# Window attention and two feed-forward stages on one core: another order in the first block, two float32 groups fewer

## The chip, the core and the metric

One core of a Trainium2 chip. Its engines are TensorE (PE; loads of weights are shown apart as PEld), VectorE (DVE), ScalarE (ACT), GpSimd (POOL) and SyncE (SP), which issues most of the transfers. Each engine works through its own instructions in a fixed order; between engines, semaphores make one wait for another. The metric is device time of the whole program in microseconds, the median of several runs.

## The reference

Attention in a window of 64 positions over 32 heads, then two feed-forward stages:

```python
scores = scale * np.matmul(q, k.transpose(0, 1, 3, 2))
mask = (rel >= 0) & (rel < window)          # rel = row - column, window = 64
attn = softmax of scores where mask, row by row
x = (attn @ v), heads side by side          # 2304 x 512
a = x @ w1                                  # 512 x 1024
b = x @ w2                                  # 512 x 1024
h = a * b @ w3                              # 1024 x 1024
x = h @ w_out                               # 1024 x 512
h = x @ w_in                                # 512 x 2048
g = h * (1.0 / (1.0 + np.exp(-h)))
return g @ w_out2                           # 2048 x 512
```

The inputs of the first stages come in double words, two 32-bit words for a number, which the kernel turns into float32 itself.

## The kernel before

The kernel writes its order out by hand; no scheduler moves anything. Nearly all of its products run with operands that are split into a high and a low part (hi and lo, a cast and a subtraction), three products for one: hi by hi, hi by lo, lo by hi.

**Phase W** (0 to 84 us) converts the weights and multiplies w3 and w_out into one matrix, which lies as eight split tiles wp[0] to wp[7]. A weight goes through steps (`steps_to`): step t scales chunk t on ACT (L168, L171), joins chunk t-1 on DVE (L200, L203) and POOL (L207), casts the high part of chunk t-3 on ACT (L214) and makes the low part of chunk t-4 (L218) on POOL or DVE. The weights w1 and w2 are the last 16 chunks; the last steps run inside block 0 of phase A. The last four accumulators of phase W (accw) are split into wp[4] to wp[7] by a cast on ACT (L127) and a subtraction on DVE (L130).

**Phase A** (84 to 450 us) has nine blocks of 256 tokens. A block is 288 products. Products 0 to 191 make 16 tiles (tile s: 12 products; ab), four tiles for each of i = 0 to 3: two for a, two for b. ACT copies a out (L739), DVE multiplies it with b (L741), and the product p is split for the pair i: its high part on ACT (L127), its low part on POOL (L130). Products 192 to 287 (x2, L757) multiply p by wp, two accumulators of 48 products each; the lines in the diff call the eight pieces of p f = 0 to 7, two for each i. All accumulators turn through four banks.

Between the products stand the **halves** of the attention, for 72 groups of two heads by 128 rows. In block 0 a half comes at products 9, 33, 57, 81, 105, 123, 141, 159, 177 and on in steps of 18. An even half of group g has the products of the scores of g, of the values of g-2 and the transposes of g-1; an odd half normalises g and prepares group g+2: for a split group a cast of q and k on ACT (L375), the low part of k on POOL (L381, two instructions) and of q on DVE (L387), and for v a cast on ACT (L396) and a low part on POOL (L399). A **plain** group, one with g < PLAIN, has none of this: its scores (L407) and values (L484 to L486) are products in float32. Block 0 begins with the even half of group 12 at its product 9.

`tick` runs before each product: it starts the halves that are due and then the `moves` put down for that product number, the last weight steps among them. `split_x` splits the next block's x. Groups 13 and 14 stand in block 0's halves at products 57 to 159.

Of the kernel before, what the change touches and what calls it, by code (L numbers as in the profile page):

```python
# [14 lines left out]
ALU = mybir.AluOpType  # L15
# [8 lines left out]
NA = 256  # L24
NBLK = T // NA
# [4 lines left out]
PLAIN = 15  # L30
# [13 lines left out]
def tile_window_attention_ffn(ctx, tc, qkv, qkp, vp, w1, w2, w3t, w_out, w_in, w_out2, out):  # L44
# [92 lines left out]
    def accumulator(name, shape):  # L137

        turn[0] = (turn[0] + 1) % converting["banks"]
        return ps.tile(shape, F32, name=name, tag=f"ps{turn[0]}")  # L140
# [568 lines left out]
    def phase_a(blk, hooks):  # L709
# [4 lines left out]
        def unit(n):  # L714
            hooks(n)

        def tick(n):
            n += 288 * blk
            halves_to(W_HALVES + halves_by(n))
            events(n)  # L720

        for s in range(16):
            i, m, j = s // 4, s // 2 % 2, s % 2
            f = 2 * i + j
            unit(s)
            fs = slice((f % 4) * 128, (f % 4 + 1) * 128)
            if j == 0:
                acc = accumulator(f"ab{blk}_{s}", [128, 512])
            for k in range(4):
                w = weights["12", (2 * m + f // 4) * 4 + k]  # L730
                for n, (l, r) in enumerate(PASSES):
                    tick(12 * s + 3 * k + n)
                    nc.tensor.matmul(  # L733
                        acc[:, j * NA : j * NA + NA], lhsT=w[l][:, fs], rhs=x[k // 2][r][:, k % 2],
                        start=(j == 0 and k == 0 and n == 0), stop=(k == 3 and n == 2), skip_group_check=True,
                    )
            if j and m == 0:
                a_sb = slot(f"a{blk}_{i}", "st", [2, 512], bufs=4)
                nc.scalar.copy(out=a_sb[:, 0], in_=acc)  # L739
            elif j:  # L740
                nc.vector.tensor_tensor(out=a_sb[:, 1], in0=acc, in1=a_sb[:, 0], op=ALU.mult)  # L741
                hi, lo = [y[:, 2 * i : 2 * i + 2] for y in p]
                split(hi, lo, a_sb[:, 1].rearrange("p (f n) -> p f n", f=2), "act", "pool")
        for i in range(2):
            acc = accumulator(f"x2_{blk}_{i}", [128, 512])
            early, late = (range(6), (6, 7)) if i == 0 else (range(8), ())
            todo = [(o, f, n) for o in range(2) for f in early for n in ((0, 0), (1, 0), (0, 1))]
            for passes in (((0, 0), (1, 0)), ((0, 1),)):
                todo += [(o, f, n) for o in range(2) for f in late for n in passes]
            for n, (o, f, (l, r)) in enumerate(todo):  # L750
                if n % 12 == 0:
                    unit(16 + 4 * i + n // 12)
                if blk + 1 < NBLK and (i, n) in ((0, 28), (1, 16)):
                    split_x(blk + 1, i)
                tick(192 + 48 * i + n)
                at = (2 * i + o) * 128
                nc.tensor.matmul(  # L757
                    acc[:, o * NA : o * NA + NA], lhsT=wp[f][l][:, at : at + 128], rhs=p[r][:, f],
                    start=(n == 0), stop=((o, f) not in [y[:2] for y in todo[n + 1 :]]), skip_group_check=True,
                )  # L760
            x2 = slot(f"x2s{blk}_{i}", "st", [2, NA], bufs=4)
            nc.scalar.copy(out=x2, in_=acc.rearrange("p (o n) -> p o n", o=2))
            nc.scalar.dma_start(
                out=x2d[2 * i : 2 * i + 2, :, blk * NA : (blk + 1) * NA].rearrange("o p n -> p o n"), in_=x2
            )
# [684 lines left out]
```

## Time and profile before

| | us |
|---|---|
| median of 3 runs | 804.27 (802.56 to 805.58) |
| profiled execution | 803.03 |
| its span, first to last instruction | 800.6 |
| PE busy | 792.2 |
| DVE, ACT, POOL busy | 632.0, 558.3, 346.0 |
| phase W | 0 to 84.2 |
| block 0 of phase A | 84.2 to 128.1 |
| block 1 | 128.1 to 170.0 |

In the trace a row has a start and a duration; matmuls are pipelined and their durations overlap, so the time that a matmul costs is the distance of starts. In brackets stands how long the engine was idle before the row, and what released it.

### The profile page before, as it was taken

To read this page: it belongs to the slowest core of one execution; us is meant where nothing else is said; L and a number is where in the kernel's file an instruction comes from. 1 tells how busy PE (TensorE), PEld (TensorE's weight loads), DVE (VectorE), ACT (ScalarE), POOL (GpSimd) and SP (SyncE) were. 2 spreads that over 40 slices of the span, in tenths; PEclk is the share of its full clock that TensorE was granted. 3 is DMA by queue.
4 is the path that set the end of the run, shared out by engine and by line. 5 is a ranking of instruction groups with operands and counts; after the bars stand their busy time and mean duration, and the time that the engine had idled before them with its cause. 6 is when DMAs were issued, how large, how long until landed. Compare 5 with 4: busy or idle time off the path is not lost.

```text
span 800.6 us, 17243 instructions
## 1 busy us (share of the span) xinstructions
PE 792.2 (99%) x5926; PEld 750.0 (94%) x5926; DVE 632.0 (79%) x1545; ACT 558.3 (70%) x1288; POOL 346.0 (43%) x416
## 2 busy tenths in 40 slices
PE   8999999999999999999999999999999999999998
PEld 4555899999999999999999999999999999999998
DVE  7898677888889888889747777847646899998882
ACT  6998868898988898888845677767657655434440
POOL 5778766777877686878533303433100000000000
PEclk9999999999999999999999999999999999999999
DMA  9998134455536554643413359789675845554421
GB/s 298 366 317 292 57 116 151 139 169 171 167 117 184 160 164 131 181 150 126 160 53 107 126 189 337 255 302 349 239 273 183 293 130 159 160 152 146 133 79 53
DMA packets 81494, 146.77 MB, mean 183 GB/s; under 512 B 7040, under 2 KB 47616, under 8 KB 81408
## 3 DMA queue, kind: packets, MB, share of 16 engines
q1 hardware_dynamic: 76352, 140.80, 54.1%
q10 hardware_dynamic: 5056, 4.88, 1.8%
q8 instruction: 47, 0.77, 0.4%
q14 instruction: 39, 0.32, 0.1%
HBM read 105.81 MB, written 39.85 MB: 182 GB/s over the span
## 4 chain that ended last, share of the span: by engine, by line
PE 84%; DVE 4%; ACT 3%; DMA 2%; issue 1%; SPq 0%; ACTq 0%; DVEq 0%
PE ab L733 23%; PE x L757 12%; PE oa L1197 10%; PE ob L1197 8%; PE ha L1046 6%; PE hd L1046 6%; PE hb L1046 6%; PE hc L1046 3%; PE t L458 3%; PE o L491 1%; PE accw L657 1%; PE s L411 1%; PE s L415 1%; DMA gst<-t 1%; PE o L492 1%
## 5 line engine op out<-in xcount | busy, mean ns | idle before, releaser
L733 PE MATMUL ab<-xb,hl 128*128 128x256 f32 x864 | 132.1, 281 | 0.0
L733 PE MATMUL ab<-xa,hl 128*128 128x256 f32 x864 | 122.1, 277 | 0.1
L733 PEld LDWEIGHTS ab<-xb,hl 128*128 128x128 f32 x864 | 112.1, 188 | 0.1
L733 PEld LDWEIGHTS ab<-xa,hl 128*128 128x128 f32 x864 | 109.4, 188 | 0.9 <-DVE wp L130 0.9
L757 PE MATMUL x<-p,wp 128*128 128x256 f32 x864 | 105.1, 278 | 0.0
L757 PEld LDWEIGHTS x<-p,wp 128*128 128x128 f32 x864 | 100.5, 188 | 0.0
L381 POOL TENSOR_TENSOR klo<-qk,qkhi 64x192 fp32r<-64x192 f32 x114 | 72.1, 632 | 4.5 <-ACT qkhi L375 0.2
L1197 PE MATMUL oa<-wo_w,hi 128*128 128x256 f32 x408 | 73.8, 276 | 0.0
L130 POOL TENSOR_TENSOR p<-a,p 128x512 fp32r<-128x512 f32 x36 | 47.9, 1330 | 38.5 <-ACT p L127 38.2
L1197 PEld LDWEIGHTS oa<-wo_w,hi 128*128 128x128 f32 x408 | 61.6, 188 | 0.0
L1197 PE MATMUL oa<-wo_w,lo 128*128 128x256 f32 x204 | 56.3, 276 | 0.0
L1046 PE MATMUL ha<-xop,wi_w 128*128 128x384 f32 x288 | 54.0, 337 | 0.0
L436 ACT ACTIVATE sm<-sm,nm 128x192 f32<-128x192 f32 x114 | 51.1, 449 | 2.8 <-DVE nm L422 1.2
L1046 PEld LDWEIGHTS ha<-xop,wi_w 128*128 128x128 f32 x288 | 50.1, 188 | 0.4 <-ACT gxa L1068 0.2
L375 ACT CAST qkhi<-qk 128x768 fp32r<-128x768 f32 x57 | 47.6, 835 | 1.3
L914 POOL TENSOR_TENSOR cv_b<-cv_b,cv_r 128x512 int32<-128x512 int32 x16 | 21.6, 1352 | 60.9 <-DVE cv_b L911 46.5
L422 DVE CUSTOM_DVE_ANT_0 sm<-s,consts 128x192 f32<-128x192 f32 x144 | 45.6, 354 | 2.9 <-PE s L415 1.1
L1046 PE MATMUL hd<-xop,wi_w 128*128 128x384 f32 x252 | 47.6, 336 | 0.0
L448 DVE TENSOR_TENSOR sm<-sm,rs 128x384 f32<-128x384 f32 x57 | 45.7, 801 | 1.9
L127 ACT CAST p<-a 128x512 fp32r<-128x512 f32 x36 | 22.4, 621 | 35.5 <-DVE a L741 35.5
L1046 PEld LDWEIGHTS hd<-xop,wi_w 128*128 128x128 f32 x252 | 44.0, 188 | 0.0
L503 POOL TENSOR_TENSOR xr<-ot 128x128 f32<-128x128 f32 x44 | 25.8, 587 | 39.9 <-DVE ot L502 31.4
(282 smaller groups left out, 2167.3 us busy)
## 6 DMA issues: line engine op xcount, KB each, us to landing
qk<-in_qkv SPq DMA_DIRECT2D x57, 384.0 KB, 3.1
gd<-gxa SPq DMA_DIRECT2D x24, 384.0 KB, 4.2
words<-in_w SPq DMA_DIRECT2D x16, 512.0 KB, 7.5
xe<-in_w_in SPq DMA_DIRECT2D x16, 512.0 KB, 5.2
gq<-in_w_out SPq DMA_DIRECT2D x16, 512.0 KB, 5.4
words<-in_w3t SPq DMA_DIRECT2D x15, 512.0 KB, 7.8
gd<-gst SPq DMA_DIRECT2D x18, 384.0 KB, 5.5
xe<-gd SPq DMA_DIRECT2D x13, 512.0 KB, 3.9
```

The source lines that it names most:

```text
L130: (nc.vector if eng_lo == "dve" else nc.gpsimd).tensor_tensor(out=lo, in0=src, in1=f32(hi), op=ALU.subtract)
L375: nc.scalar.copy(out=hi, in_=t)
L381: nc.gpsimd.tensor_tensor(out=k_lo[g % 2][hs, h * 192 : h * 192 + 192], in0=t[hs, n], in1=f32(hi[hs, n]), op=ALU.subtract)
L422: nc.vector.tensor_tensor_reduce(out=sm[g % 2][:, h, :], in0=s_ps[:, h, :], in1=consts[:, at + 64 - 64 * h : at + 256 - 64 * h], op0=ALU.a ...
L436: nc.scalar.activation(out=e[:, h, :], in_=x, func=AF.Exp, scale=-1.0, bias=nm[:, h : h + 1], accum_out=sums_of[g % 2][:, h, 0:1])
L448: nc.vector.tensor_tensor(out=x, in0=e, in1=rs.unsqueeze(2).to_broadcast([128, 2, 192]), op=ALU.mult)
L458: nc.tensor.transpose(t_ps[:, i * 128 : i * 128 + 128], x[:, at : at + 128], id_sb)
L503: nc.gpsimd.tensor_tensor(out=to, in0=t[:, 0:128], in1=t[:, 128:256], op=ALU.add)
L733: nc.tensor.matmul(acc[:, j * NA : j * NA + NA], lhsT=w[l][:, fs], rhs=x[k // 2][r][:, k % 2], start=(j == 0 and k == 0 and n == 0), stop= ...
L757: nc.tensor.matmul(acc[:, o * NA : o * NA + NA], lhsT=wp[f][l][:, at : at + 128], rhs=p[r][:, f], start=(n == 0), stop=((o, f) not in [y[: ...
L1046: nc.tensor.matmul(bank[name][:, q, 0:NB], lhsT=w[:, l, first + kt], rhs=x[:, kt, r, :], start=(fresh and kt == 0 and n == 0), stop=(kt == ...
L1197: nc.tensor.matmul(dst, lhsT=lhs[l], rhs=rhs[r], start=(first and e == 0 and q == 0 and n == 0), stop=(e == DUOS - 1 and q == 1 and n == 2 ...
```

## The change

Float32 groups go from 15 to 13: groups 13 and 14 are split like all that follow. Block 0 does its tiles in two portions: tiles 0 to 7, then the x2 products that need only p of these (48 of 96), then tiles 8 to 15 and the other 48. Both x2 accumulators are then open through the second portion, and its tiles turn through the two banks left. In each portion the x2 products of the second pair come last, first those that read the high part of p (LEFT), then those with its low part (RIGHT). Blocks 1 to 8 keep their order. The seven weight steps of block 0 stand at products 15, 39, 63, 87, 97, 111 and 129 instead of 15, 27, 43, 60, 68, 79 and 107, and the low part of the last goes from DVE to POOL.

```diff
-PLAIN = 15
+PLAIN = 13
...
-    def accumulator(name, shape):
-
-        turn[0] = (turn[0] + 1) % converting["banks"]
+    def accumulator(name, shape, of=(0, 1, 2, 3)):
+
+        turn[0] = of[(of.index(turn[0]) + 1) % len(of)] if turn[0] in of else of[0]
         return ps.tile(shape, F32, name=name, tag=f"ps{turn[0]}")
...
+        def ab_tiles(units, banks=(0, 1, 2, 3)):
+            for s in units:
...
+                for k in range(4):
+                    w = weights["12", (2 * m + f // 4) * 4 + k]
+                    for n, (l, r) in enumerate(PASSES):
+                        tick()
...
+                elif j:
+                    nc.vector.tensor_tensor(out=a_sb[:, 1], in0=acc, in1=a_sb[:, 0], op=ALU.mult)
+                    hi, lo = [y[:, 2 * i : 2 * i + 2] for y in p]
+                    split(hi, lo, a_sb[:, 1].rearrange("p (f n) -> p f n", f=2), "act", "pool")
...
+        def x2_tiles(*todo):
+            for i, o, f, (l, r) in todo:
+                if i not in acc2:
+                    acc2[i] = accumulator(f"x2_{blk}_{i}", [128, 512])
+                tick()
...
+        ALL, LEFT, RIGHT = ((0, 0), (1, 0), (0, 1)), ((0, 0), (1, 0)), ((0, 1),)
+
+        def some(i, fs, passes):
+            return [(i, o, f, n) for o in range(2) for f in fs for n in passes]
+
+        if blk:
+            ab_tiles(range(16))
+            x2_tiles(*some(0, range(6), ALL), *some(0, (6, 7), LEFT), *some(0, (6, 7), RIGHT), *some(1, range(8), ALL))
+            return
+        for g in range(2):
+            f = 4 * g
+            ab_tiles(range(8 * g, 8 * g + 8), (0, 1, 2, 3) if g == 0 else [n for n in range(4) if n not in held])
+            x2_tiles(*some(0, (f, f + 1), ALL), *some(1, (f, f + 1), ALL))
+            held = (turn[0], (turn[0] - 1) % 4)
+            for i in range(2):
+                x2_tiles(*some(i, (f + 2, f + 3), LEFT), *some(i, (f + 2, f + 3), RIGHT))
+        turn[0] = held[0]
...
-        for i, n in enumerate((15, 27, 43, 60, 68, 79, 107)):
-            low = nc.vector if i == 6 else nc.gpsimd
-            moves.setdefault(n, []).append(lambda i=i, low=low: steps_to(W12_B + 25 + i, (low,)))
+        for i, n in enumerate((15, 39, 63, 87, 97, 111, 129)):
+            moves.setdefault(n, []).append(lambda i=i: steps_to(W12_B + 25 + i, (nc.gpsimd,)))
```

How instructions stand on three engines, before and after (the number behind a name is the program's own for the buffer, and line numbers of the changed kernel differ by some).

ACT at the end of phase W, before: the last two chunks are scaled (words), then the four accumulators are cast into wp.

```order
L214 CAST hl<-cv_b 128x512
L168 ACTIVATE cv_b<-words 128x512
L171 ACTIVATE cv_r<-words 128x512
L168 ACTIVATE cv_b<-words 128x512
L171 ACTIVATE cv_r<-words 128x512
L127 CAST wp_971<-accw_0_640 128x512
L127 CAST wp_975<-accw_1_641 128x512
```

The same place on ACT after:

```order
L214 CAST hl<-cv_b 128x512
L168 ACTIVATE cv_b<-words 128x512
L171 ACTIVATE cv_r<-words 128x512
L168 ACTIVATE cv_b<-words 128x512
L171 ACTIVATE cv_r<-words 128x512
L375 CAST qkhi_969<-qk_904 128x768
L127 CAST wp_980<-accw_0_640 128x512
L127 CAST wp_984<-accw_1_641 128x512
```

The cast of q and k of group 13 now stands ahead of the casts of wp.

POOL in block 0, before, up to the low part of p for the second pair (p from a_1): L207 and L218 are sums and low parts of weights, klo the low part of k.

```order
L207 TENSOR_TENSOR cv_b<-cv_b,cv_r 128x512 x2
L218 TENSOR_TENSOR hl<-cv_b,hl 128x512
L207 TENSOR_TENSOR cv_b<-cv_b,cv_r 128x512
L218 TENSOR_TENSOR hl<-cv_b,hl 128x512
L130 TENSOR_TENSOR p_994<-a_0_1049,p_994 128x512
L207 TENSOR_TENSOR cv_b<-cv_b,cv_r 128x512
L218 TENSOR_TENSOR hl<-cv_b,hl 128x512 x3
L381 TENSOR_TENSOR klo_80<-qk_1077,qkhi_1183 64x192 x2
L130 TENSOR_TENSOR p_994<-a_1_1165,p_994 128x512
```

POOL after, from the low part of k of group 14 to the same low part of p:

```order
L381 TENSOR_TENSOR klo_79<-qk_906,qkhi_1073 64x192 x2
L207 TENSOR_TENSOR cv_b<-cv_b,cv_r 128x512
L218 TENSOR_TENSOR hl<-cv_b,hl 128x512
L130 TENSOR_TENSOR p_1003<-a_0_1058,p_1003 128x512
L207 TENSOR_TENSOR cv_b<-cv_b,cv_r 128x512
L218 TENSOR_TENSOR hl<-cv_b,hl 128x512
L381 TENSOR_TENSOR klo_80<-qk_974,qkhi_1182 64x192 x2
L399 TENSOR_TENSOR vhl_1184<-v_1080,vhl_1184 128x3x64
L207 TENSOR_TENSOR cv_b<-cv_b,cv_r 128x512
L218 TENSOR_TENSOR hl<-cv_b,hl 128x512
L130 TENSOR_TENSOR p_1003<-a_1_1167,p_1003 128x512
```

Two low parts of weights have moved behind p; the low parts of a second group's k and of a v have come ahead of it.

PE before, around product 120 (ab_8 and ab_10 are tiles 8 to 11; s, o and t are the scores, values and transposes of the half at product 105):

```order
L733 MATMUL ab_8_1209<-xa_570,hl 128x256 x6
L733 MATMUL ab_8_1209<-xb_833,hl 128x256 x3
L407 MATMUL s_1219<-kq_81 128x384
L484 MATMUL o_1226<-pw_127,vp_83 128x128
L485 MATMUL o_1226<-pw_127,vp_83 128x128
L486 MATMUL o_1226<-pw_127,vp_83 128x64
L458 MATMUL t_1231<-consts,sm_78 128x128 x3
L733 MATMUL ab_8_1209<-xb_833,hl 128x256 x3
L733 MATMUL ab_8_1209<-xa_570,hl 128x256 x6
L733 MATMUL ab_8_1209<-xb_833,hl 128x256 x6
L733 MATMUL ab_10_1257<-xa_570,hl 128x256 x6
```

PE after, from shortly ahead of product 120 (the third row) on:

```order
L759 MATMUL x_0_1_1261<-p_1003,wp_594 128x256 x3
L759 MATMUL x_0_1_1261<-p_1003,wp_598 128x256 x3
L759 MATMUL x_0_0_1219<-p_1003,wp_629 128x256 x2
L759 MATMUL x_0_0_1219<-p_1003,wp_633 128x256 x2
L759 MATMUL x_0_0_1219<-p_1003,wp_629 128x256 x2
L759 MATMUL x_0_0_1219<-p_1003,wp_633 128x256 x2
L759 MATMUL x_0_0_1219<-p_1003,wp_629 128x256
L759 MATMUL x_0_0_1219<-p_1003,wp_633 128x256
L759 MATMUL x_0_0_1219<-p_1003,wp_629 128x256
L759 MATMUL x_0_0_1219<-p_1003,wp_633 128x256
L759 MATMUL x_0_1_1261<-p_1003,wp_629 128x256 x2
```

Where tiles 10 and 11 stood, PE now has x2 products of the second pair: eight with p's high part, then four, from product 128, with its low part.

## Rows read from the trace of the kernel before

**Rows 1.** The page, busy time by engine and granted clock in slices
```profile
PE 792.2 (99%) x5926; PEld 750.0 (94%) x5926; DVE 632.0 (79%) x1545; ACT 558.3 (70%) x1288; POOL 346.0 (43%) x416
...
PE   8999999999999999999999999999999999999998
...
PEclk9999999999999999999999999999999999999999
```

**Rows 2.** The page, chain that ended last, shares by engine
```profile
PE 84%; DVE 4%; ACT 3%; DMA 2%; issue 1%; SPq 0%; ACTq 0%; DVEq 0%
```

**Rows 3.** Timeline of PE, three halves; start us, us, engine, line, instruction
```profile
99.49 0.81 PE L407 MATMUL s<-kq 128*128 128x384 f32 x2
...
101.00 0.60 PE L733 MATMUL ab<-xb,hl 128*128 128x256 f32 x3
...
105.35 0.37 PE L411 MATMUL s<-qkhi 128*128 128x192 f32 x2
...
106.62 0.60 PE L733 MATMUL ab<-xb,hl 128*128 128x256 f32 x3
...
116.27 0.37 PE L411 MATMUL s<-qkhi 128*128 128x192 f32 x2
...
117.27 4.36 PE L757 MATMUL x<-p,wp 128*128 128x256 f32 x36
```

**Rows 4.** Timeline of PE, products 120 to 131 of block 0
```profile
102.81 0.84 PE L733 MATMUL ab<-xa,hl 128*128 128x256 f32 x6
103.49 0.99 PE L733 MATMUL ab<-xb,hl 128*128 128x256 f32 x6
```

**Rows 5.** Timeline of all engines, from phase W to block 0
```profile
82.86 2.01 ACT L127 CAST wp<-accw 128x512 fp32r<-128x512 f32 x4
...
83.45 2.48 DVE L130 TENSOR_TENSOR wp<-accw,wp 128x512 fp32r<-128x512 f32 x4
84.19 0.77 PEld L733 LDWEIGHTS ab<-xa,hl 128*128 128x128 f32 x6 [0.92 <-DVE wp L130]
```

**Rows 6.** Timeline of ACT in block 0
```profile
90.28 0.57 ACT L739 COPY a<-ab 128x512 f32<-128x512 f32 x1
...
115.35 0.83 ACT L375 CAST qkhi<-qk 128x768 fp32r<-128x768 f32 x1
116.08 0.35 ACT L396 CAST vhl<-v 128x192 fp32r<-128x192 f32 x1
```

**Rows 7.** Timeline of POOL in block 0, up to p of the second pair
```profile
91.48 1.30 POOL L207 TENSOR_TENSOR cv_b<-cv_b,cv_r 128x512 int32<-128x512 int32 x1 [1.83 <-DVE rs L444]
92.73 1.29 POOL L218 TENSOR_TENSOR hl<-cv_b,hl 128x512 fp32r<-128x512 f32 x1
...
98.99 3.96 POOL L218 TENSOR_TENSOR hl<-cv_b,hl 128x512 fp32r<-128x512 f32 x3
102.91 1.60 POOL L381 TENSOR_TENSOR klo<-qk,qkhi 64x192 fp32r<-64x192 f32 x2
104.59 1.29 POOL L130 TENSOR_TENSOR p<-a,p 128x512 fp32r<-128x512 f32 x1
```

**Rows 8.** Timeline of DVE in block 0, weight step and low part of q
```profile
92.11 0.69 DVE L200 TENSOR_SCALAR cv_z<-cv_b 128x512 int32<-128x512 int32 x1
92.89 0.69 DVE L203 SCALAR_TENSOR_TENSOR cv_b<-words,cv_z 128x512 int32<-128x512 int32 x1
...
100.44 1.34 DVE L387 TENSOR_TENSOR qkhi<-qk,qkhi 64x256 fp32r<-64x256 f32 x1 [2.00 <-ACT qkhi L375]
...
106.05 0.42 DVE L387 TENSOR_TENSOR qkhi<-qk,qkhi 64x256 fp32r<-64x256 f32 x1 [0.26 <-ACT qkhi L375]
```

**Rows 9.** Timeline of POOL after the half at product 213 of block 0
```profile
119.85 1.55 POOL L130 TENSOR_TENSOR xa<-xr,xa 128x512 fp32r<-128x512 f32 x1 [0.94 <-ACT xa L127]
...
122.02 1.27 POOL L381 TENSOR_TENSOR klo<-qk,qkhi 64x192 fp32r<-64x192 f32 x2
123.37 0.61 POOL L399 TENSOR_TENSOR vhl<-v,vhl 128x192 fp32r<-128x192 f32 x1
```

More of the change, by code (lines that the diff above doesn't have):

```diff
@@ L712, in phase_a, with tick @@
         p = [t[:, i : i + 8 * NA].rearrange("p (f n) -> p f n", f=8) for i in (48, 2096)]
-        def unit(n):
-            hooks(n)
-        def tick(n):
+        count = [0]
+        def tick():
+            n = count[0]
+            count[0] += 1
+            if n % 12 == 0:
+                hooks(n // 12)
+            if blk + 1 < NBLK and n in (220, 256):
+                split_x(blk + 1, n // 256)
             n += 288 * blk
@@ L720, in tick @@
             events(n)
[L722 to L735, printed above, removed]
-                    )
[L737 to L765, printed above, removed]
@@ new lines, in ab_tiles @@
+        def ab_tiles(units, banks=(0, 1, 2, 3)):
+            for s in units:
+                i, m, j = s // 4, s // 2 % 2, s % 2
+                f = 2 * i + j
+                fs = slice((f % 4) * 128, (f % 4 + 1) * 128)
+                if j == 0:
+                    acc = accumulator(f"ab{blk}_{s}", [128, 512], banks)
+                for k in range(4):
+                    w = weights["12", (2 * m + f // 4) * 4 + k]
+                    for n, (l, r) in enumerate(PASSES):
+                        tick()
+                        nc.tensor.matmul(
+                            acc[:, j * NA : j * NA + NA], lhsT=w[l][:, fs], rhs=x[k // 2][r][:, k % 2],
+                            start=(j == 0 and k == 0 and n == 0), stop=(k == 3 and n == 2), skip_group_check=True,
+                        )
+                if j and m == 0:
+                    a_sb = slot(f"a{blk}_{i}", "st", [2, 512], bufs=4)
+                    nc.scalar.copy(out=a_sb[:, 0], in_=acc)
+                elif j:
+                    nc.vector.tensor_tensor(out=a_sb[:, 1], in0=acc, in1=a_sb[:, 0], op=ALU.mult)
+                    hi, lo = [y[:, 2 * i : 2 * i + 2] for y in p]
+                    split(hi, lo, a_sb[:, 1].rearrange("p (f n) -> p f n", f=2), "act", "pool")
@@ new lines, in phase_a @@
+        acc2, left = {}, [48, 48]
+        def x2_tiles(*todo):
[3 more added lines that the diff above has]
+                tick()
+                at = (2 * i + o) * 128
+                left[i] -= 1
+                nc.tensor.matmul(
+                    acc2[i][:, o * NA : o * NA + NA], lhsT=wp[f][l][:, at : at + 128], rhs=p[r][:, f],
+                    start=(left[i] == 47), stop=(left[i] == 0), skip_group_check=True,
+                )
+                if left[i] == 0:
+                    x2 = slot(f"x2s{blk}_{i}", "st", [2, NA], bufs=4)
+                    nc.scalar.copy(out=x2, in_=acc2[i].rearrange("p (o n) -> p o n", o=2))
+                    nc.scalar.dma_start(
+                        out=x2d[2 * i : 2 * i + 2, :, blk * NA : (blk + 1) * NA].rearrange("o p n -> p o n"), in_=x2
+                    )
```

## The prediction

> **What bounds the kernel now.** I read the page first, from its busy line to the chain that ended last. [...] So this kernel's time is the sum of what PE streams plus the few gaps in it: an edit gains only what it takes from PE's own work or from PE's waits, and it loses whatever it makes PE wait. The other engines have no price of their own, but each of them is a queue in strict order, and what PE reads comes out of them. The profiled execution took 803.03 us, 2.43 outside its span; it lies 1.24 below the median of the three runs, 804.27. I make the sum against 803.03 and add 1.24 at the end.
>
> The change acts between 82 and 131 us: the end of phase W and block 0 of phase A. From block 1 on the order is the old one, so a shift at block 1's start goes through to the end unchanged. Next I read PE's timeline there, and then the queues of ACT, DVE and POOL.
>
> **What PE saves: two float32 groups.** A half's stop in the product stream costs PE 1.51 us where group and values are float32 (99.49 to 101.00), 1.27 where the scores are split and the values still float32 (105.35 to 106.62), and 1.00 where all is split (116.27 to 117.27) [rows 3]. So split scores save 0.24 and split values 0.27. With PLAIN at 13 the stops at products 57 and 105 get split scores, and those at 141 and 177 split values: 2 x 0.24 + 2 x 0.27 = 1.02 us less, 0.48 of it ahead of product 128.
>
> **The steps moved to products 15 to 129.** In block 0 the stream has one gap of its own: six products that take 0.84 elsewhere take 0.99 at 103.49 [rows 4], where the last weight's low part, the step at 107, has only just been written by DVE. In the new order these weights are first read at product 144 and later, the last one at 179, fifty products after its step at 129. Fifty products at 0.114 are 5.7 us, so I take that 0.15 back and put no cost on the later steps: what hides them is the 24 x2 products and the 24 after them that now stand in front. Moving the low part of step 129 from DVE to POOL adds 1.29 to POOL [rows 7], behind the last thing PE waits for in the first half of the block.
>
> **Where the ab products start.** Group 13 is no longer float32, so its preparation at the end of phase W is now a cast of 768 columns on ACT, which the order puts directly ahead of the four casts of wp; on DVE its low part of q comes ahead of the four low parts of wp. ACT is not idle there: the casts of wp start at 82.86, DVE's first low part follows at 83.45, and PE's first ab product, whose bank the latter frees, starts at 84.19 after its weights waited 0.92 [rows 5]. The cast holds ACT for 0.73 (115.35 to the start of the next row at 116.08) [rows 6]. All three move by that: ab starts at 84.92, **+0.73**. The lower end is the same 0.73, since nothing stands between cast and casts; the upper end is 1.65, if DVE's low part of q takes 1.34 in place of 0.42 [rows 8] because POOL is in an instruction.
>
> **Product 128, the main term.** After tile 7 PE now does 24 x2 products with the first two pairs, then 8 with the high parts of the next pair (from product 120), then 4 with their low parts, from product 128. In the old order product 128 was an ab product, which needs no p at all. When does PE get there? It was at 126 at 103.49 [rows 4], so at 128 at 103.72; less the 0.48 saved so far, plus 0.73: **103.97**. When is the low part of this p (call it p1) ready? POOL writes it, and the order shows what stands ahead of it on POOL. The chain starts on ACT: the copy of the first a stood at 90.28 [rows 6], now at 91.01; group 14's cast comes right behind it (0.57 and 0.83: done at 92.41). DVE's low part of q takes 0.42 more (92.83), the two DVE steps of the weight conversion 0.78 and 0.69 [rows 8]: 94.30. From there POOL has, in order, a sum, a low part, p0's low part, a sum, a low part (7 with the sum and the low part that follow), group 15's two low parts of k, its low part of v, and only then p1. The seven cost 1.25 each by the distance of starts (91.48 to 92.73), 1.32 in the row of three (3.96): I take 1.28, so 8.96; k's pair is 1.60 [rows 7], v's 0.61 [rows 9]. 94.30 + 8.96 + 2.21 = 105.47, and p1's own 1.29 gives **106.76**. PE waits 106.76 - 103.97 = **2.8 us** here. (Part of it falls at product 120 already, for the high part; the sum is one.) In the old order the same instruction ended at 105.88 [rows 7] and hurt nobody, because its first reader stood behind tile 15. Low end: seven at 1.25 and a pair of k at 1.27 [rows 9], 2.2 us. High end: DVE's low part of q at 1.34, 3.9 us. I take 2.8, by the row of the same queue at the same place.
>
> **Product 272, the same once more.** The last pair's low part (p3) is wanted by product 272, 32 products behind tile 15 where the old order left 44. Counted from the stop at product 213 (116.27 in the old trace): PE needs 59 x 0.114 + 2 x 1.00 = 8.7 us to get there. POOL works on that half's and the next block's low parts from 3.58 to 7.71 us after the stop (119.85 to 123.98) [rows 9]; ahead of this stands now a copy of a on ACT, 0.5 by its 0.57, and behind it p3's 1.29: ready after 9.5. Wait: **0.75 us**, between 0.3 (the copy hidden) and 1.5 (both DVE low parts slow).
>
> **Edits with no price.** Two loads of 384 KB in place of four of 80 KB go ahead of a v and two weight loads on SP's queue; those weights are now read at products 39 and 63, many us later, and if that cover went, the casts of ACT would wait for the landing. Only two banks turn in the second half of block 0, so each has 24 products (2.7 us) and mostly one stop to be emptied; ACT's copy takes 0.57. That fails only if ACT is behind by over 2 us, and then the wait is part of the rival below. Float32 values of 13 and 14 fall away and with them two copies on ACT; the split groups put more on ACT, DVE and POOL, which is in the chains above.
>
> **The sum.** -1.02 - 0.15 + 0.73 + 2.8 + 0.75 = **+3.1 us** (bounds +1.9 and +4.9). 803.03 + 3.1 = 806.1; with 1.24, **807.4** against a median of 804.27, 0.39% more. A measurement of this kernel can tell 0.5%, 4.0 us, from no change: the likeliest case is inside that, on the slow side.
>
> **Rivals.**
> First, **slower by more than 0.5%**: DVE and POOL hinder each other. The same DVE instruction takes 0.42 when POOL starts behind it and 1.34 when POOL is in the middle of one [rows 8], and POOL's pair of k takes 1.60 at one place and 1.27 at another [rows 7, 9]. The change adds two such DVE instructions and two pairs, and on POOL's unbroken queue up to p1 the first is far likelier to meet a running instruction. Price: +0.9 at group 14, +0.2 on POOL for group 15, and +0.7 at p3: 4.9 in all, **809.2**. It decides from 0.9 more than my sum. [...]
> Second, **everything is hidden**: POOL reaches p1 in time, because its input comes earlier than I think or fewer low parts stand ahead. Then -1.17 + 0.73 = -0.4, 803.8. The order speaks against it: eleven instructions of known length stand there, and the old row already ends at 105.88, 1.9 past the time of need.
> [...]
>
> **How the numbers follow.** Forecast (806 to 808.2): 0.60. First rival: 0.28. Hidden: 0.09. Clock: 0.03. Faster by over 0.5% would need 4 us, where PE's own saving is 1.2: 0.02, from scatter alone. Within 0.5%: the forecast and the hidden case, 0.68. Slower: 0.30. Range: the lower bound of the sum, 806.2, less 1.2 for the scatter of the runs (802.56 to 805.58): 805.0; the upper bound 809.2 and 0.5: 809.7.
>
> **What would show each step.** In the changed profile: stops of 1.27, 1.27, 1.00 and 1.00 at products 57, 105, 141 and 177; the first ab product 0.7 to 1.7 later; a wait of PE on p's high part at an x2 product after tile 7 and a longer one on POOL directly behind it, 2 to 4 us together; one of 0.3 to 1.5 behind tile 15; no gap on weights in tiles 8 to 15; blocks 1 to 8 as long as before. I am wrong if PE runs through product 128, if the ab products wait for weights, or if a later block changes its length.

## The result: 809.46 us, 0.66% slower, and the profile after

The changed kernel takes 809.46 us, the median of six runs (808.26 to 811.56), against 804.25 for the kernel before: a ratio of 1.0066, 95% interval 1.0048 to 1.0083. So it is slower, by 5.2 us. In five more runs it took 808.69, 4.5 us more than before. The prediction had 807.4 in a range of 805.0 to 809.7: the time lies inside, near the top, and outside the likeliest case's own 806 to 808.2. I had given 0.30 to "slower by over 0.5%". The profile is of the longest of the six executions, 811.56; the lengths of its blocks 0 and 1 come back in a second profile, of an execution of 808.62.

Three rows of the changed kernel's page answer to [rows 1, 2], on which the reading of PE as the bound rests: busy time by engine, the granted clock in slices, and the engines' shares of the chain.

```profile
PE 794.2 (98%) x5922; PEld 751.0 (93%) x5922; DVE 636.2 (79%) x1556; ACT 561.4 (69%) x1298; POOL 351.6 (43%) x425
...
PEclk9999999999999999999999999999999999999999
...
PE 68%; ACT 7%; DVE 6%; issue 3%; DMA 2%; POOL 2%; SPq 0%; ACTq 0%; DVEq 0%; POOLq 0%
```

PE has less of the chain: its share falls from 84% to 68%, and ACT, DVE and POOL together rise from 7% to 15%. The list of waits of PE says where (engine, line, waited for, us in total, times, longest):

```profile
PE x L759 <- POOL p L130: 2.4, 2, 1.5
...
PE t L458 <- DVE sm L448: 1.5, 4, 0.5
```

In the timeline of PE these stand in block 0 so (start us, us, engine, line, instruction, in brackets the idle time ahead and its releaser):

```profile
86.21 0.95 PE L738 MATMUL ab<-xa,hl 128*128 128x256 f32 x6 [1.39 <-DVE wp L130]
...
94.43 0.37 PE L411 MATMUL s<-qkhi 128*128 128x192 f32 x2
...
95.69 0.60 PE L738 MATMUL ab<-xb,hl 128*128 128x256 f32 x3
...
102.51 1.97 PE L759 MATMUL x<-p,wp 128*128 128x256 f32 x15
105.41 1.21 PE L759 MATMUL x<-p,wp 128*128 128x256 f32 x8 [0.93 <-ACT p L127]
108.15 1.76 PE L759 MATMUL x<-p,wp 128*128 128x256 f32 x13 [1.53 <-POOL p L130]
109.75 0.36 PE L411 MATMUL s<-qkhi 128*128 128x192 f32 x2
...
126.30 2.86 PE L759 MATMUL x<-p,wp 128*128 128x256 f32 x23
130.02 1.77 PE L759 MATMUL x<-p,wp 128*128 128x256 f32 x13 [0.87 <-POOL p L130]
...
133.06 0.85 PE L738 MATMUL ab<-xa,hl 128*128 128x256 f32 x6
```

A bracket counts from the modelled end of the product before, so it is 0.2 to 0.3 us shorter than the delay by the distance of starts, which I use for the sums (0.93 for 1.19, 1.53 for 1.83, 0.87 for 1.10).

**Products 120 and 128.** From 102.51 fifteen products at 0.114 end at 104.22; the next, which needs the high part of p1, starts at 105.41, 1.19 later. Its eight products would end at 106.32; the first with the low part starts at 108.15, 1.83 later. Together 3.02. The rows of ACT and POOL that end the two waits:

```profile
104.73 0.62 ACT L127 CAST p<-a 128x512 fp32r<-128x512 f32 x1 [2.94 <-DVE a L746]
```

```profile
106.83 1.26 POOL L130 TENSOR_TENSOR p<-a,p 128x512 fp32r<-128x512 f32 x1
```

The low part is the end of POOL's queue, which runs without a break from 95.68. The high part, the first wait, is not POOL's own row: ACT's cast waits for DVE's product of a and b (104.02), ahead of which DVE had a low part of q that took 1.48 and two instructions of a weight step.

**Product 272.** 126.30 and 23 products at 0.114 make 128.92; the low part of p3 lets it start at 130.02: 1.10.

**The stops** at products 57 (94.43 to 95.69), 105, 141 and 177 take 1.26, 1.26, 0.99 and 0.99, where they took 1.51, 1.51, 1.27 and 1.27: 1.06 saved. Block 0 takes 46.85 from first to first ab product (86.21 to 133.06), before 43.89: 2.96 more, and 3.02 + 1.10 - 1.06 - 0.15 (the old gap of [rows 4], which is gone) is 2.91.

**The first ab product.** The all-engine timeline of the changed kernel at the end of phase W, the place of [rows 5]:

```profile
83.55 0.83 ACT L375 CAST qkhi<-qk 128x768 fp32r<-128x768 f32 x1
...
83.88 1.27 POOL L207 TENSOR_TENSOR cv_b<-cv_b,cv_r 128x512 int32<-128x512 int32 x1
...
84.28 2.06 ACT L127 CAST wp<-accw 128x512 fp32r<-128x512 f32 x4
84.42 1.02 DVE L387 TENSOR_TENSOR qkhi<-qk,qkhi 64x256 fp32r<-64x256 f32 x1 [0.29 <-ACT qkhi L375]
...
85.47 1.29 DVE L130 TENSOR_TENSOR wp<-accw,wp 128x512 fp32r<-128x512 f32 x2
```

The cast costs ACT the expected 0.73 (83.55 to 84.28). But DVE's low part of q starts while POOL is in an instruction (83.88 to 85.15) and takes 1.02 in place of 0.42. DVE's low parts of wp, which free PE's bank, so start 1.05 behind its own start and not behind ACT's cast. Counted from the last scores product of phase W, here and then in the kernel before,

```profile
74.41 0.88 PE L407 MATMUL s<-kq 128*128 128x384 f32 x2 [0.45 <-PE accw L657]
```

```profile
73.68 0.88 PE L407 MATMUL s<-kq 128*128 128x384 f32 x2 [0.45 <-PE accw L657]
```

the first ab product comes 11.80 later (86.21) in place of 10.51 (84.19): **1.29** more, where I had 0.73.

**Block 1 is longer too**: 42.61 us (133.06 to 175.67) in place of 41.87 (128.08 to 169.95). PE waits there twice for DVE's normalised scores (before, once, for 0.23):

```profile
153.76 0.52 PE L458 MATMUL t<-consts,sm 128*128 128x128 f32 x3 [0.40 <-DVE sm L448]
...
164.63 0.52 PE L458 MATMUL t<-consts,sm 128*128 128x128 f32 x3 [0.30 <-DVE sm L448]
```

I had put no cost on anything behind block 0.

### The profile page after: what moved, and what is told of

The parts are those of the page before. It is cut to its first block, busy times and chain, and to the rows that moved or that the text cites. A ratio compares the mean times of both kernels' runs of the same rounds, so it can differ in the third digit from the quotient of the medians.

```text
span 809.8 us, 17273 instructions
## 1 busy us (share of the span) xinstructions
PE 794.2 (98%) x5922; PEld 751.0 (93%) x5922; DVE 636.2 (79%) x1556; ACT 561.4 (69%) x1298; POOL 351.6 (43%) x425
## 4 chain that ended last, share of the span: by engine, by line
PE 68%; ACT 7%; DVE 6%; issue 3%; DMA 2%; POOL 2%; SPq 0%; ACTq 0%; DVEq 0%; POOLq 0%
PE ab L738 15%; PE oa L1217 11%; PE x L759 8%; PE ob L1217 8%; PE ha L1066 6%; PE hd L1066 6%; PE hb L1066 6%; PE hc L1066 3%; PE t L458 2%; ACT sm L436 1%; DMA gst<-t 1%; PE o L491 1%; DMA xe<-in_w_in 1%; PE s L411 1%; PE s L415 1%
## 5 line engine op out<-in xcount | busy, mean ns | idle before, releaser
L381 POOL TENSOR_TENSOR klo<-qk,qkhi 64x192 fp32r<-64x192 f32 x118 | 74.2, 629 | 6.5 <-ACT qkhi L375 2.1
L436 ACT ACTIVATE sm<-sm,nm 128x192 f32<-128x192 f32 x118 | 52.8, 449 | 2.4 <-DVE nm L422 0.8
L375 ACT CAST qkhi<-qk 128x768 fp32r<-128x768 f32 x59 | 49.3, 835 | 1.3
L501 DVE TENSOR_TENSOR ot<-o,ot 64x256 f32<-64x256 f32 x59 | 24.6, 417 | 24.8 <-ACT ot L500 24.3
```

The source lines that it names most:

```text
L375: nc.scalar.copy(out=hi, in_=t)
L381: nc.gpsimd.tensor_tensor(out=k_lo[g % 2][hs, h * 192 : h * 192 + 192], in0=t[hs, n], in1=f32(hi[hs, n]), op=ALU.subtract)
L436: nc.scalar.activation(out=e[:, h, :], in_=x, func=AF.Exp, scale=-1.0, bias=nm[:, h : h + 1], accum_out=sums_of[g % 2][:, h, 0:1])
L501: nc.vector.tensor_tensor(out=t[0:64], in0=o_ps[0:64, 0, :], in1=t[0:64], op=ALU.add)
```

## The experiments

All edits but those of before_plain13 and before_again are made on the changed kernel. The table gives the two lengths in each profile (block 0: from its first ab product to block 1's; block 1 likewise) and the median time.

| kernel | block 0 | block 1 | median us (runs) | ratio to before |
|---|---|---|---|---|
| before | 43.89 | 41.87 | 804.25 (6) | |
| before_again | 43.86 | 41.85 | 804.12 (1) | |
| changed | 46.85 | 42.61 | 809.46 (6) | 1.0066 (1.0048 to 1.0083) |
| after_again | 46.91 | 42.63 | 808.69 (5) | 1.0062 (1.0050 to 1.0075) |
| order_plain15 | 45.86 | 42.66 | 805.77 (11) | 1.0022 (1.0013 to 1.0031) |
| before_plain13 | 49.60 | 41.87 | 811.04 (4) | 1.0085 (1.0071 to 1.0099) |
| prep13_late | 46.83 | 42.63 | 809.09 (5) | 1.0060 (1.0047 to 1.0074) |
| x2_copy_dve | 48.30 | 41.96 | 808.20 (4) | 1.0050 (1.0035 to 1.0065) |
| steps_behind_p1 | 45.49 | 42.61 | 807.06 (5) | 1.0039 (1.0025 to 1.0053) |
| p1_dve | 45.66 | 42.63 | 807.29 (4) | 1.0044 (1.0029 to 1.0059) |
| right_last | 45.54 | 43.51 | 809.15 (1) | |
| old_steps | 50.71 | 42.65 | 812.44 (1) | |
| combo13 | 44.68 | 42.77 | 805.68 (12) | 1.0024 (1.0013 to 1.0035) |
| combo15 | 44.00 | 42.97 | 803.49 (12) | 0.9998 (0.9988 to 1.0007) |

### What recurs

> The changed kernel once more, for what recurs. Its first trace has block 1 start 4.98 us later than before: 0.72 of it is there already at 14 us (phase W), 1.30 comes at the first ab product, 2.96 at products 120 and 128, 0.98 at product 272, and 1.17 is saved. Blocks 1 and 2 are 0.74 and 0.70 longer (waits on DVE's normalised scores), and a wait of 1.7 with a lower granted clock stands at 645 us. Theory A: only the waits of block 0 belong to the change. Then those three recur within 0.3 us, the 0.72 and what stands at 645 do not, the median is 808.5 to 809.5. Theory B: the waits in blocks 1 and 2 belong to it too, handed on by engines that leave block 0 late. Then they recur as well, about 1 us. Rival: all of it is scatter of transfers; then the waits of block 0 differ by more than 1 us between the two traces.

> The kernel before, profiled a second time, to tell what of the differences is scatter. Theory A: block 0 takes 43.9 and block 1 41.9 again within 0.1 us, and phase W may end up to 1 us later or earlier than in the first profile (its first products wait for loads). Rival: the blocks themselves scatter by 0.7 us or more; then the waits seen in block 1 of the changed kernel mean nothing.

The second profile of the changed kernel, timeline of PE:

```profile
105.37 1.21 PE L759 MATMUL x<-p,wp 128*128 128x256 f32 x8 [0.93 <-ACT p L127]
108.11 1.78 PE L759 MATMUL x<-p,wp 128*128 128x256 f32 x13 [1.53 <-POOL p L130]
```

The waits come back to the hundredth, at the first ab product (1.39), at 120 and 128 and at 272 (0.87), and to 0.03 in block 1 (0.37 and 0.32); the kernel before has its 43.9 and 41.9 again. Theory B holds for block 1: its 0.75 belongs to the change. Block 2 does not: 42.18 in the first profile, 41.56 in the second, 41.48 twice before. What is there at the end of phase W is scatter: the last scores product of phase W starts at 73.68 and 74.77 in the two profiles of before, and the 0.7 by which the changed kernel's first profile is late there means nothing.

### The parts of the change, one at a time

> The new order and the new step places, with 15 float32 groups as before. Theory A (the waits come from the two split groups' preparations that stand ahead of p1 on POOL and ahead of wp on ACT and DVE): ab starts as before, POOL has 3.6 us less ahead of p1 (two pairs of k at 1.5, one v at 0.6), so the wait at 128 is at most 1 us, that at 272 stays near 1: 0.6 to 1.9 us above before, 805 to 806. Rival: the order itself costs it (x2 is too early whatever POOL has ahead): waits of 3 and 1 as in the changed kernel and no PE time saved: 808 or more.

```diff
-PLAIN = 13
+PLAIN = 15
```

The timeline of PE with the new order, the new step places and 15 float32 groups:

```profile
104.76 1.74 PE L759 MATMUL x<-p,wp 128*128 128x256 f32 x13 [0.72 <-POOL p L130]
```

805.77, inside what theory A gave (805 to 806): without the two groups' preparations the wait at 120 is gone, the one at 128 is 0.72 and nothing is late at the first ab product; the one at 272 stays (0.86). But block 1 is 42.66 here too. So the loss in block 1 comes from the order, not from the groups. (Blocks 0 and 1 are 2.8 longer in this profile, the median 1.6; 0.4 of the difference is time outside the span, see below, the rest was not traced.)

> The old order and the old step places, with 13 float32 groups. Theory A: PE saves 1.02, ab starts 1.30 later as in the changed kernel, and POOL gets two pairs of k and two v more while the last weights' low parts are made; these are read from product 96 on, so the wait moves to ab products of tiles 8 to 11 and is 2 to 4 us: 2.3 to 4.3 above before, 806.5 to 808.6. Rival, the float32 groups are a gain that the order spoils: 1.0 below before plus at most 0.7 for the cast, 803.2 to 804.

```diff
-PLAIN = 15
+PLAIN = 13
```

(made on the kernel before). Its timeline of PE, and the busy times by stretch with the granted clock (PE, PEld, DVE, ACT, POOL busy with instructions, PEclk, DMA share, GB/s):

```profile
106.49 0.39 PE L733 MATMUL ab<-xa,hl 128*128 128x256 f32 x1 [0.61 <-POOL hl L218]
...
107.91 0.62 PE L733 MATMUL ab<-xb,hl 128*128 128x256 f32 x3 [0.80 <-POOL hl L218]
111.57 0.58 PE L733 MATMUL ab<-xb,hl 128*128 128x256 f32 x1 [3.04 <-DVE hl L218]
```

```profile
112.00:114.00 2.00, 2.00 (x11) 2.00 (x11) 1.08 (x2) 0.35 (x1) 1.46 (x2) 0.50 0.00 0
```

The waits fall on ab products, as theory A said, but they are 4.45 in all, over its upper end of 4, and behind the last of them the granted clock is 0.50 (112 to 114 us): 811.04 in place of 806.5 to 808.6. So fewer float32 groups alone cost 6.9 us, the new order with its step places alone 1.6, both together 4.5 to 5.2: the order takes back a part of what the two groups cost, and neither is a gain.

> The changed kernel with the old step places (15, 27, 43, 60, 68, 79, 107) and the last low part on DVE. Theory A (queues): two more sums and low parts, 5 us of POOL, stand ahead of p0 and p1; the wait at 120 and 128 grows to 4 or more, and one appears at the first x2 products: block 0 48 to 50 us. Rival, the prediction's own price of nothing on the step places: 46.9 as in the changed kernel.

```diff
-        for i, n in enumerate((15, 39, 63, 87, 97, 111, 129)):
-            moves.setdefault(n, []).append(lambda i=i: steps_to(W12_B + 25 + i, (nc.gpsimd,)))
+        for i, n in enumerate((15, 27, 43, 60, 68, 79, 107)):
+            low = nc.vector if i == 6 else nc.gpsimd
+            moves.setdefault(n, []).append(lambda i=i, low=low: steps_to(W12_B + 25 + i, (low,)))
```

Timeline of PE:

```profile
102.10 1.09 PE L759 MATMUL x<-p,wp 128*128 128x256 f32 x7 [1.15 <-POOL p L130]
107.81 1.21 PE L759 MATMUL x<-p,wp 128*128 128x256 f32 x8 [1.55 <-ACT p L127]
```

Waits at the first x2 products, at 120 (1.55) and 128 (1.65), block 0 at 50.71, a granted clock of 0.68 from 112 to 116: theory A, a little over its upper end. The later steps are a needed part of the new order: without them block 0 of this one profile is 3.9 us longer, the clock's part included.

### The terms of the sum, one at a time

> The changed kernel, with group 13's preparation (cast, low parts, the loads behind it) put behind the casts and low parts of wp. Theory A: ab starts 1.30 us earlier, relative to the end of the last accumulators, and all behind it moves along, since what feeds POOL's queue up to p1 starts from the first copy of a: block 1 starts 1.3 earlier, 808.2. Rival: POOL's queue hangs on the weight steps, not on the ab products; then p1 is ready as late as before, the wait at 128 grows by 1.3 and the time stays at 809.5.

```diff
-            lows = prep_qk(g + 2)
...
+            if g == 11:
+                late13.append(lambda: after_norm(g))
+            else:
+                after_norm(g)
...
         phase_w()
+        late13.pop()()
```

(after_norm holds the lines taken out.) All engines at the start of block 0, the casts of wp being done ahead of these rows:

```profile
85.15 0.98 PE L746 MATMUL ab<-xa,hl 128*128 128x256 f32 x6
...
85.68 0.88 ACT L375 CAST qkhi<-qk 128x768 fp32r<-128x768 f32 x1
```

The first ab product comes 10.52 behind the last scores product (85.15 against 74.63), as before the change, and block 0 stays at 46.83: so the 1.29 is this preparation, and POOL's queue up to p1 does start from the first copy of a. The time does not follow: 809.09, where 808.2 was expected. In the profiled run the gain is gone again by the last stage, through 0.4 us in block 2, a wait of 0.42 at 484 us and 0.3 in the last stage, places that differ from profile to profile. Five runs do not tell whether that is scatter or a loss that follows; it stays open.

> The changed kernel with the weight steps of products 87, 97 and 111 at 99, 111 and 123. Theory A (queues up to p1): the step of 87 takes 1.4 us of DVE out of the way of the second a*b, and its sum and low part, 2.5 us, stand behind p1 on POOL: of the 2.96 us at products 120 and 128 at most 0.7 is left. Part comes back at product 144, whose weights' low parts are now made later, up to 1.5: block 1 starts 0.8 to 2.3 us earlier. Rival: POOL's work up to the second half of the block is the bound whatever its order; then the whole wait moves to product 144 and the time does not change.

```diff
-        for i, n in enumerate((15, 39, 63, 87, 97, 111, 129)):
+        for i, n in enumerate((15, 39, 63, 99, 111, 123, 129)):
```

Timeline of PE:

```profile
106.38 1.74 PE L759 MATMUL x<-p,wp 128*128 128x256 f32 x13 [0.32 <-POOL p L130]
113.98 0.38 PE L738 MATMUL ab<-xb,hl 128*128 128x256 f32 x1 [0.80 <-POOL hl L218]
```

The wait at 120 is gone, 0.32 is left at 128, 0.80 comes back at the weights of the second portion: block 0 is 1.4 shorter, within theory A's 0.8 to 2.3. The edit moves the two DVE instructions of the step at 87 out of the way of the product of a and b, and its two POOL instructions behind p1. So the step's place in these two queues was the cause; how much each queue made is not shown by this run. POOL's total work takes part of the gain back.

> The changed kernel with p1's low part in block 0 on DVE in place of POOL. Theory A: ACT's high part is done 0.63 behind its start at 104.7, DVE follows with 0.7 to 1.3: low part ready at 106.1 to 106.7 in place of 108.1, so the second wait (1.53) is gone or nearly, the first (0.93, for the high part) stays: block 1 starts 1.3 to 1.8 us earlier, 807.0 to 807.4. Rival: DVE has no room: the scores' chain of the next halves falls behind by that 0.7 to 1.3 and PE waits for it at the transposes; then less than 0.7 is gained.

```diff
-                    split(hi, lo, a_sb[:, 1].rearrange("p (f n) -> p f n", f=2), "act", "pool")
+                    split(hi, lo, a_sb[:, 1].rearrange("p (f n) -> p f n", f=2), "act", "dve" if blk == 0 and i == 1 else "pool")
```

Timeline of DVE, and of PE:

```profile
105.25 0.80 DVE L130 TENSOR_TENSOR p<-a,p 128x512 fp32r<-128x512 f32 x1 [0.68 <-ACT p L127]
```

```profile
105.27 2.67 PE L759 MATMUL x<-p,wp 128*128 128x256 f32 x21 [0.92 <-ACT p L127]
109.02 0.52 PE L458 MATMUL t<-consts,sm 128*128 128x128 f32 x3 [0.33 <-ACT vhl L396]
```

The low part is done at 106.05, and PE runs 21 products without a break; the wait of 1.53 is gone. 0.33 comes back at the transposes, so block 0 gains 1.2 where 1.3 to 1.8 was expected; the median, 807.29, is inside the 807.0 to 807.4.

> The changed kernel with the high parts of p for both accumulators ahead of the low parts, in both portions. Eight more products, 0.91 us, then stand between the first need of p's high part and that of its low part. If POOL's queue sets p's low part and does not start from these products, the waits at product 128 and 272 shrink by 0.91 each: block 0 45.1 in place of 46.9. If not, the wait moves along and block 0 stays at 46.9.

```diff
-            for i in range(2):
-                x2_tiles(*some(i, (f + 2, f + 3), LEFT), *some(i, (f + 2, f + 3), RIGHT))
+            for n in (LEFT, RIGHT):
+                x2_tiles(*some(0, (f + 2, f + 3), n), *some(1, (f + 2, f + 3), n))
```

Timeline of PE:

```profile
108.87 0.86 PE L759 MATMUL x<-p,wp 128*128 128x256 f32 x5 [0.64 <-POOL p L130]
110.62 0.52 PE L458 MATMUL t<-consts,sm 128*128 128x128 f32 x3 [0.16 <-DVE sm L448]
```

The wait at 128 shrinks from 1.53 to 0.64, 0.89 less for eight products, and that at 272 is gone: POOL's queue does not hang on these products. Block 0 is 1.3 shorter (1.8 expected, 0.16 comes back at the transposes), but block 1 is 0.9 longer still, 43.51: both x2 accumulators now end within the last products of the block.

### What makes block 1 longer

> The changed kernel; block 0's first x2 accumulator is copied out by DVE in place of ACT, and SP issues its store. Theory A: block 1's two waits on the normalised scores (0.37 and 0.32, together 0.75 of length) come from this copy and its issue, 1.04 us of ACT, which the new order puts at the block's end, where ACT has no idle time (in the old order it stood ten us earlier beside some). Then block 1 takes 41.9 in place of 42.63 and the time falls by 0.7. Rival: the lag comes out of block 0's longer queues on DVE and POOL and is carried on; then block 1 stays at 42.6, or grows, as DVE has 0.7 more.

```diff
-                    nc.scalar.copy(out=x2, in_=acc2[i].rearrange("p (o n) -> p o n", o=2))
-                    nc.scalar.dma_start(
+                    early = blk == 0 and i == 0
+                    (nc.vector.tensor_copy if early else nc.scalar.copy)(out=x2, in_=acc2[i].rearrange("p (o n) -> p o n", o=2))
+                    (nc.sync if early else nc.scalar).dma_start(
```

What is taken from ACT, in the changed kernel's timeline of ACT (ACTq is its DMA issue):

```profile
132.24 0.58 ACT L765 COPY x2s<-x 128x512 f32<-128x512 f32 x1
132.84 0.40 ACTq L766 DMA_DIRECT2D x2d<-x2s  x1
133.29 0.68 ACT L238 ACTIVATE cv_r<-xe 128x512 int32<-128x512 uint32 x1 [0.48 <-ACT x2s L765]
```

The same copy in the kernel before:

```profile
121.82 0.58 ACT L762 COPY x2s<-x 128x512 f32<-128x512 f32 x1
```

From the copy to the next instruction ACT is held for 1.05. In the old order this copy ends the first accumulator at product 239 and starts at 121.82, 6 us ahead of the block's end; in the new one it stands in the last microsecond of block 0. ACT's last idle time ahead of it is 0.96 us up to 127.27, so it hands the delay to the exponentials and so to DVE's normalised scores. ACT's next cast of transposes (L468) shows the lag: it starts 0.81 behind block 1's first product (133.87), where it stood 0.16 ahead of it before (127.92 against 128.08). With the copy on DVE it is 0.10 ahead again, and block 1 takes 41.96: theory A, the 0.75 was this copy. Block 0 of this profile is 1.4 longer than in the changed kernel, for another reason, but that is not what let ACT catch up: block 0 of old_steps is longer still, with the copy on ACT, and its block 1 takes 42.65. Timeline of PE, then busy times and clock by stretch:

```profile
108.52 3.14 PE L759 MATMUL x<-p,wp 128*128 128x256 f32 x13 [1.53 <-POOL p L130]
```

```profile
108.00:110.00 2.00, 1.48 (x7) 1.48 (x8) 1.88 (x3) 1.52 (x4) 2.00 (x3) 0.56 0.00 0
110.00:112.00 2.00, 2.00 (x12) 2.00 (x12) 1.51 (x2) 0.00 (x0) 2.00 (x2) 0.59 0.04 8
```

Behind the same two waits as in the changed kernel (0.93, eight products, 1.53) the granted clock is down at 0.56 and 0.59 here: the thirteen products up to the stop take 2.94 (108.52 to 111.46), where they took 1.60 in the changed kernel's own profile (108.15 to 109.75). That is the fall of the clock to which I had given 0.03, with a price of 1.34, in one of the three profiles whose rows show these two waits; in the changed kernel's two the clock is 1.00 from 108 to 112 us.

### All of it together

> The changed kernel with four edits together: group 13's preparation behind wp; the weight steps of 87, 97 and 111 at 97, 111 and 123, the low part of the first of these on DVE; in each portion the high parts of p for both accumulators ahead of the low parts; block 0's first x2 copied by DVE. If the losses are the waits named so far (1.3 at the first ab product, 3.0 at 120 and 128, 1.1 at 272, 0.75 in block 1), most of 6.2 goes and the 1.17 of PE time that 13 groups save stays: block 1 starts 42.7 to 43.9 us after the first ab product (46.9 in the changed kernel, 43.9 before), the clock stays at full speed there, and the time is 802.5 to 804.5, at the level of before. If the load of the two split groups on POOL and DVE is the bound whatever the order, block 0 stays over 45 and the time over 805.5.

> The same without the first edit, with 15 float32 groups and all low parts on POOL. By the waits alone: nothing saved on PE but the 0.15 gap, no wait left at 120 to 128, at most 0.3 at product 272, block 1 as long as before: block 0 43.7 to 44.2, time 803.9 to 804.6. If the order itself costs, 805.8 as in the run with the new order and 15 groups.

combo13 has the edits of prep13_late, right_last and x2_copy_dve, and

```diff
-        for i, n in enumerate((15, 39, 63, 87, 97, 111, 129)):
+        for i, n in enumerate((15, 39, 63, 97, 111, 123, 129)):
+            low = nc.vector if i in (3,) else nc.gpsimd
...
```

combo15 has those of right_last, x2_copy_dve and steps_behind_p1, and 15 float32 groups.

combo13, timelines of DVE and of PE:

```profile
104.67 1.59 DVE L218 TENSOR_TENSOR hl<-cv_b,hl 128x512 fp32r<-128x512 f32 x1
```

```profile
109.21 0.52 PE L458 MATMUL t<-consts,sm 128*128 128x128 f32 x3 [1.19 <-DVE sm L448]
```

No wait on p is left, but the low part that DVE took over holds it for 1.59, and PE waits 1.19 for the scores behind it: block 0 is 44.68, between the two theories, and the time, 805.68, over the 802.5 to 804.5 expected. It is 0.24% over before, where the changed kernel is 0.6% over: the named waits explain most of the loss. That the load of two more groups on the three engines keeps the rest is likely, not shown: combo15, without it, differs in more than the groups. (combo13's profile is of the longest of its twelve executions, 809.83; its mean granted clock is 0.995: it is 0.91 from 640 to 660 us and 1.00 in blocks 0 and 1, and the eight accw products at 10.52 us take 5.40, in combo15's profile 3.70.)

combo15 gives 0.9998 (0.9988 to 1.0007): the new order without its waits is as good as the old one and no better. Its block 0 is the 43.7 to 44.2 expected, its block 1 is not: 42.97. So DVE's copy does not bring block 1 back with the low parts last in both accumulators. There the copy starts 0.4 behind block 1's first product (131.34 against 130.91 in combo13, 127.59 against 127.23 in combo15), where in x2_copy_dve it starts 0.5 ahead of it (134.35 against 134.89); whether that is the reason is not shown. Nor is it shown why the 1.2 us by which blocks 0 and 1 of combo15 are longer do not appear in its median; some 0.3 is time outside the span. None of these versions beats the kernel before.

## Why the prediction was right and where it was not

| step | predicted, us | measured, us |
|---|---|---|
| stops of the groups | -1.02 | -1.06 |
| gap of the last weight | -0.15 | -0.15 |
| first ab product | +0.73 (to 1.65) | +1.29 |
| products 120 and 128 | +2.8 (2.2 to 3.9) | +3.02 |
| product 272 | +0.75 (0.3 to 1.5) | +1.10 |
| block 1 | 0 | +0.75 |
| sum | +3.1 | +4.95 |

The main step was right in cause and close in size: p1 had to wait for POOL's queue, and it was ready 21.88 us behind the first ab product (86.21 to 108.09, POOL's own row being 106.83 with 1.26), where the rows of before had given 21.84. The parts fit as well as the sum: POOL's queue starts 9.47 behind the first ab product (95.68), forecast 9.38, and takes 12.41 up to the end of p1, forecast 12.46. Right too: the four stops, no gap on weights in tiles 8 to 15, the wait at 272 in its cause. Its size, 1.10 for 0.75, comes mostly from the copy of a on ACT ahead of the next block's low parts. I had it at 0.5 us, and POOL starts on them 4.37 us after the stop at 213 (120.13 to 124.50) in place of 3.58, so 0.79 later:

```profile
124.50 1.29 POOL L130 TENSOR_TENSOR xa<-xr,xa 128x512 fp32r<-128x512 f32 x1 [0.89 <-ACT xa L127]
```

Mis-sized was the **first ab product**: I took the lower end, ACT's 0.73, and put DVE's slow low part of q into the first rival at group 14. There it took 0.42; it was slow at group 13, in phase W (84.42 + 1.02 = 85.44, POOL's 83.88 + 1.27 = 85.15), and at groups 15 and 16. Each time DVE's instruction ended 0.28 or 0.29 behind the end of the POOL instruction it had met, as these rows and two more of the changed kernel's DVE and two of its POOL show (101.02 + 1.29 = 102.31 and 101.11 + 1.48 = 102.59; 108.06 + 2.86 = 110.92 and 109.80 + 1.40 = 111.20):

```profile
101.11 1.48 DVE L387 TENSOR_TENSOR qkhi<-qk,qkhi 64x256 fp32r<-64x256 f32 x1 [1.20 <-POOL cv_b L207]
...
109.80 1.40 DVE L387 TENSOR_TENSOR qkhi<-qk,qkhi 64x256 fp32r<-64x256 f32 x1
```

```profile
101.02 1.29 POOL L218 TENSOR_TENSOR hl<-cv_b,hl 128x512 fp32r<-128x512 f32 x1
...
108.06 2.86 POOL L218 TENSOR_TENSOR hl<-cv_b,hl 128x512 fp32r<-128x512 f32 x2
```

All 59 such DVE instructions of this trace fit: 17 start inside a POOL instruction, of which ten take 0.48 to 1.48 and end 0.28 or 0.29 behind its end, and the seven that start within its last 0.1 us take 0.42; the 42 others start ahead of a POOL instruction and take 0.42 as well. So which of the two times of [rows 8] comes depends here on which of the two instructions starts first, and on how much of POOL's is then left. Of the first rival 0.56 us came at the first ab product, none at the place where I had put its 0.9.

That the time still lies in the range is in part luck. The range's top is the first rival's 809.2 and 0.5, and what brought the time there was largely not that rival but block 1, the 272 term and the clock, less a gain outside the span (both below). The sum's bounds were also added wrongly: the terms' own ends (0.73 to 1.65, 2.2 to 3.9, 0.3 to 1.5) give +2.1 and +5.9, not +1.9 and +4.9, and the measured +4.95, block 1's 0.75 in it, lies inside the right ones and just outside mine.

Wrong was **"blocks 1 to 8 as long as before"**. Among the edits with no price I had looked at the two banks that turn in the second portion, and not at the two that the x2 accumulators hold and at what it costs to empty them: the first x2 accumulator's copy and issue, 1.05 us of ACT, moved from beside idle time to the block's last microsecond. This is the step that failed outright, 0.75 us, shown by x2_copy_dve.

Two things lie outside the sum. The **clock**: I gave its fall 0.03 as a case by itself, an estimate that rested on no run. In the runs it is rather a surcharge that some of them pay, 1.34 us in block 0 of x2_copy_dve. The mean granted clock is under 0.999 in 6 of the changed kernel's 11 runs (down to 0.995), in 3 of 5 of prep13_late and 4 of 4 of before_plain13; in steps_behind_p1, p1_dve, order_plain15 and combo15, where the waits at 128 are shorter or gone, in none of 32, and in none of 46 runs of before. The changed kernel's five runs at 0.999 or 1.000 have spans of 806.3 to 807.2 us, the six others 807.3 to 809.8. Where the fall stands is shown in block 0 for three kernels' profiles (x2_copy_dve, before_plain13, old_steps); in the changed kernel's first profile it stands at 648 us instead, behind waits of 0.53 and 0.91 us on the last weights, and no profile of the changed kernel shows one in block 0. So it is likely, and not shown, that its other runs pay at the waits of block 0. The two stretches at 648 us:

```profile
644.00:648.00 4.00, 2.44 (x17) 1.85 (x15) 4.00 (x8) 4.00 (x8) 0.00 (x0) 1.00 0.33 102
648.00:652.00 4.00, 3.75 (x19) 3.55 (x18) 3.93 (x11) 2.21 (x5) 0.00 (x0) 0.57 0.28 96
```

Right behind these waits the granted clock is 0.57 (648 to 652 us); the profile's forty slices of 20 us, all 9, hide it. And the **time outside the span**: 2.2 to 2.6 us in every run of before, 1.7 to 1.9 in every run with 13 groups, 1.9 to 2.2 with the new order and 15. This gain of some 0.6 I did not foresee; why it comes is not shown. Together: 4.95 at the first ab product and in blocks 0 and 1, less 0.6, plus nothing to some 3 for the clock by run, where 5.2 and 4.5 were measured as medians.

## What to carry to other kernels

Where PE is the bound and reads through strict queues, ask of a moved product which queue writes its operand and add up what stands ahead there, with durations from that same place: this gave the main wait as 2.8 us where 3.02 was measured. Then look at the other end of the same move: what the products release, and which engine has to empty it at the new place without idle time. And weigh a saving on PE against the work that it puts on other engines where their queues already reach PE: here 1.02 us saved on PE cost 6.9 us in the old order and some 3 in the new one.

## What the runs showed of the hardware that was not expected

DVE's low part of q does not slow down by a factor when it meets a running POOL instruction: it ends 0.28 to 0.29 us behind POOL's end (0.42 where it starts first; 1.02, 1.48 and 1.40 at the end of phase W and in block 0), and in the kernel before as well: its row of 1.34 in [rows 8] ends at 101.78, and the POOL instruction that it met, the second of the row of three in [rows 7], at 101.50. The granted clock fell to 0.56 behind two waits of 0.93 and 1.53 us with eight products between them in one profile (x2_copy_dve) and stayed at 1.00 in two others with the same waits to the hundredth (the changed kernel's).
